# A planned last stage: banks counted as taken, and the planner's constants set anew

## The chip, the cores and the metric

One core of a Trainium2 chip. The metric is device time in microseconds of one execution; smaller is better. TensorE does matrix products, VectorE and ScalarE elementwise work with access to the accumulator memory PSUM (eight banks, each 128 partitions x 512 fp32), GpSimd elementwise work in SBUF only, SyncE issues the transfers.

## The reference

Three layers, one after the other, on 3072 tokens of width 512, fp32 in and out:

```python
attn  = softmax(mask(q @ k.T / 8)) @ v          # 4 batches, 8 heads, window 128 and 4 sinks
x     = attn as (3072, 512)
d     = softmax(x @ phi, over tokens)           # 32 slots
slots = relu((d.T @ x)[e] @ w1[e]) @ w2[e]      # 8 experts, 4 slots each
x     = softmax(x @ phi, over slots) @ slots
h     = x @ w_in                                # (512, 2048)
out   = (h - tanh(h)) @ w_out                   # (2048, 512)
```

## The kernel before

Attention and the experts come first and are written out by hand; the change leaves them alone. The last stage computes `out`, transposed, in three chunks of 1024 tokens. Because x is a combination of 32 slots, h for a tile of 128 of the 2048 columns (an f of 16) and 512 tokens is a single matmul (L1554) of a small precomputed matrix with the slot weights `cT`. What is large is the product with `w_out`. Each fp32 operand is split into a rounded part and a residual (`gh` and `gl` for activations, `whi` and `wlo` for weights), and three of the four cross products are summed.

The work on one tile of h, each step one instruction on 128x512:

1. TensorE makes h in one of four PSUM banks: `h0`, `h1`, `y`, `cvt` (L1554).
2. ScalarE takes tanh in place (L1565) and a scaled square into `u` (L1566).
3. VectorE multiplies the two (L1313), back into the bank or out into a spare buffer (`w`, `wf`, `g`, `cv` and others).
4. ScalarE casts the result to `gh` (L1623).
5. `gl` is the rest (L1477): by VectorE if the source is a bank, by GpSimd if it is a buffer.
6. TensorE multiplies into the accumulators `a0` to `a3` (named `o` in the profile, L1485).

The first chunk of 1024 tokens runs as 32 regular units of twelve matmuls (4 blocks of output rows x 3 cross products), called "r". The second and third run by a scheme with seven products in place of eight of half size (`MULT`: P1 to P7): a unit is one product for one f, six matmuls, and units of two products alternate (`PAIRS`). Its operands are four tiles for each i of 8 (`A11`, `A12`, `A21`, `A22`) and their sums `S1` to `S4`, made by VectorE (L1477) from banks and buffers. A bank with A22, A11 or A12 is thus read by ScalarE (cast) and by VectorE (sums, residual), and comes free when the last reader is done. On the weight side sums of `w_out` blocks are needed too (`T1` to `T4`); those for T3 and T4 are made once in the first chunk, while the last weights are still being converted and split, and those for T1 and T2 are split afresh (`trhi`, `trlo`) when they are used.

The regular units up to the sixth are written out by hand. From 256 us on the order is planned by a program at build time, in two steps:

- A loop over a heap of dated events (`produce`, `act`, `mul`, `cast`, `ssum`, `unit`, `t_fresh`) gives out banks, buffers and the five `gh`/`gl` pairs, and enters each instruction as a task with a wanted time `at`. The constants set these times, in planned us: h is asked for `LEAD` ahead of its unit (L1561, `push(max(at + 0.3, due[gs[j + 1]] - LEAD), ...)`), the cast of a regular tile `RCAST` and that of a sum `SCAST` ahead, the split of a T1 or T2 weight `TCAST` ahead. The weight sums for T3 and T4 come `TLAG` after the conversion of their weight, the last three `TLAG2` later each.
- `_Order.emit` lists the tasks: again and again it takes, over all engines, the task that can start first by its planned durations (`US`), and of those that could start at the same moment on one engine the one with the smallest `at`. A task can start when those that it depends on are done (dependencies are kept by name of bank or buffer: a read waits for the write before, a write for the write and all reads before). Two readers of one bank have no dependency. The order in which tasks were taken is the order in which the instructions stand in the engines' queues, which are in order. `BUSY` and `shared` stand for engines still at work from before and for sums that VectorE and GpSimd can't run side by side.

What waits for what at run time is then set by semaphores that the framework puts in from the tiles' reads and writes, not by the planner.

Of the kernel before, what the change touches and what calls it, by code (L numbers as in the profile page):

```python
# [19 lines left out]
PSUM = bass.MemoryType.PSUM  # L20
# [37 lines left out]
CT = ((1, 0), (1, 1), (1, 2))  # L58
EPS_T = 0.0
US = {"tanh": 0.49, "mm": 0.2276, "h": 0.232, "act": 1.1, "cast": 0.49, "cast2": 0.3, "v": 0.6, "vs2": 0.34, "p": 1.26, "p2": 0.7, "pc": 0.7, "pch": 0.38, "ev": 0.49, "sq": 0.56}  # L60
LEAD, RCAST, SCAST, TCAST = 10.0, 7.0, 4.5, 6.0
RPS = 11
GGAP = 1.4
TLAG = 14.0
TLAG2 = 2.0
PAIRS = (((1, "P4"), (1, "P5")), ((1, "P7"), (1, "P1")), ((1, "P6"), (1, "P2")), ((1, "P3"), (2, "P4")),
         ((2, "P5"), (2, "P1")), ((2, "P7"), (2, "P6")), ((2, "P2"), (2, "P3")))
# [78 lines left out]
class _Order:  # L146

    LAT = {"PE": 0.2, "SP": 4.0, "ACT": 0.11, "DVE": 0.09, "POOL": 0.05}
    SELF = {"ACT": 0.12, "DVE": 0.12, "POOL": 0.12}
    BUSY = {"ACT": 0.3, "DVE": 2.7, "POOL": 3.8}  # L150

    def __init__(self):
# [12 lines left out]
    def emit(self, near_end=0, mark=None, busy=True):  # L165
        tasks = sorted(self.tasks, key=lambda t: t[:2])
        n = len(tasks)
        wrote, read = {}, {}
        deps, users = [set() for _ in tasks], [[] for _ in tasks]
        for k, (_, _, _, rd, wr) in enumerate(tasks):  # L170
            for b in rd:
                if b in wrote:
                    deps[k].add(wrote[b])
            for b in wr:
                if b in wrote:
                    deps[k].add(wrote[b])
                deps[k] |= read.get(b, set())
            for b in rd:
                read.setdefault(b, set()).add(k)
            for b in wr:  # L180
                wrote[b], read[b] = k, set()
        for k, d in enumerate(deps):
            d.discard(k)
            for j in d:
                users[j].append(k)
        left = [len(d) for d in deps]
        avail, free = [{} for _ in tasks], dict(self.BUSY) if busy else {}
        ready = {k for k in range(n) if not left[k]}
        order, port = [], 0.0
        while len(order) < n:  # L190
            best = None
            engs = {e for k in ready for e in tasks[k][2]}
            for eng in engs:
                t0 = free.get(eng, 0.0)
                at = {}
                for k in ready:
                    if eng in tasks[k][2]:
                        x = max([t0] + [v if e != eng else v - 0.06 - self.LAT.get(e, 0.0) + self.SELF.get(e, 0.0) for e, v in avail[k].items()])
                        if self.shared(tasks[k], eng) and x < port:
                            x = port if eng == "POOL" or x < port - 0.08 else port + 0.02  # L200
                        at[k] = x
                first = min(at.values())
                k = min(k for k in at if at[k] <= first + EPS_T)
                c = (at[k], tasks[k][2][eng][0], eng, k)
                best = c if best is None else min(best, c)
            t, us, eng, k = best
            ready.remove(k)
            free[eng] = t + us
            if self.shared(tasks[k], eng):
                port = t + us  # L210
            done = t + us + 0.06 + self.LAT.get(eng, 0.0)
            order.append((k, eng))
            for j in users[k]:
                avail[j][eng] = max(avail[j].get(eng, 0.0), done)
                left[j] -= 1
                if not left[j]:
                    ready.add(j)
            self.log.append((t, us, eng, tasks[k][0], tasks[k][3], tasks[k][4]))
        for x, (k, eng) in enumerate(order):
            if mark and n - x == near_end:  # L220
                mark()
            tasks[k][2][eng][1]()
# [5 lines left out]
def tile_kernel(ctx: ExitStack, tc: tile.TileContext, qk, vv, v0, v0t, nw, phi, w1, w2,  # L228
# [17 lines left out]
    def run(ctx, fast):  # L246
# [1540 lines left out]
        for s, todo in plan.items():  # L1787
# [3 lines left out]
            for e, (f, ph) in enumerate(todo):  # L1791
# [12 lines left out]
                else:  # L1804
# [7 lines left out]
                    if f >= 8:  # L1812
# [6 lines left out]
                        def tsub(at, d, dn, a, b, rd):  # L1819
                            arith(at, d, a, b, rd, dn, half=True)  # L1820

                        tb += TLAG if f < 13 else TLAG + TLAG2 * (f - 12)
                        tsub(tb, B1[:, lo_], [l_], B1[:, hi_], B1[:, lo_], [r_, l_])
# [130 lines left out]
```

## Time and profile before

| | |
|---|---|
| median of 3 runs | 516.47 us (516.26 to 517.09) |
| the profiled execution | 516.18 us |
| its span, first to last instruction | 514.4 us |
| TensorE busy | 484.3 us, 94% of the span |
| VectorE busy | 420.5 us, 82% |
| ScalarE busy | 384.6 us, 75% |
| GpSimd busy | 297.4 us, 58% |

The profile names the engines PE (TensorE; PEld its weight loads), DVE (VectorE), ACT (ScalarE), POOL (GpSimd) and SP (SyncE). A row of the timeline gives start, duration, engine, line, operation, output<-inputs by name with the buffer number left out, and the idle time of the engine just before with what ended it. Matmuls are pipelined: each shows about 0.4 us, but the next may start 0.23 us later.

### The profile page before, as it was taken

What the parts mean: (1) busy time and instruction counts of PE and PEld (TensorE: products, weight loads), DVE (VectorE), ACT (ScalarE), POOL (GpSimd) and SP (SyncE); (2) the same over time, 40 slices, a digit from 0 to 9 for tenths busy, and PEclk for the clock granted to TensorE, in tenths of its full rate; (3) what the DMA queues carried; (4) which work ended last, traced back from release to release, by engine and by line L of the source; (5) the groups of instructions that cost most, each with busy time, mean ns of one, the idle gap of its engine ahead of it and who ended that gap; (6) DMA issues with size and microseconds to landing.
All of it is one profiled execution on the core that took longest, in us unless ns stands there. A gap on an engine that the chain in (4) does not pass through costs nothing. (4 is left out here: it accounts for less than half of the span.)

```text
span 514.4 us, 10274 instructions
## 1 busy us (share of the span) xinstructions
PE 484.3 (94%) x3554; PEld 334.8 (65%) x3554; DVE 420.5 (82%) x841; ACT 384.6 (75%) x1088; POOL 297.4 (58%) x362
## 2 busy tenths in 40 slices
PE   8799999899998999799999999999999999999995
PEld 4565565555555633236788788888788778878784
DVE  2999998898988559678999999788967887883983
ACT  4989998998999414238897887898866898574751
POOL 0466755765744100014999996167645884579952
PEclk9999999999999999999999999999999999999998
DMA  8989977442385899992432001120000030100022
GB/s 297 413 320 349 362 273 252 150 142 94 114 287 183 312 326 409 410 408 95 148 98 82 1 0 43 41 83 1 1 0 0 2 123 1 41 1 1 1 83 85
DMA packets 21996, 77.60 MB, mean 151 GB/s; under 512 B 2867, under 2 KB 4019, under 8 KB 20019
## 3 DMA queue, kind: packets, MB, share of 16 engines
q1 hardware_dynamic: 21938, 76.89, 40.6%
q8 instruction: 29, 0.48, 0.4%
q14 instruction: 29, 0.23, 0.1%
HBM read 70.59 MB, written 6.29 MB: 149 GB/s over the span
## 5 line engine op out<-in xcount | busy, mean ns | idle before, releaser
L1485 PE MATMUL o<-gh,whi 128*128 128x512 f32 x232 | 91.9, 396 | 0.0
L1485 PE MATMUL o<-gh,wlo 128*128 128x512 f32 x232 | 91.1, 393 | 0.0
L1485 PE MATMUL o<-gl,whi 128*128 128x512 f32 x232 | 71.3, 391 | 0.0
L705 POOL TENSOR_TENSOR w<-w,su 128x528 f32<-128x528 f32 x38 | 41.4, 1090 | 51.1 <-DVE su L702 36.2
L1477 POOL TENSOR_TENSOR gl<-w,gh 128x512 fp32r<-128x512 f32 x39 | 51.0, 1316 | 30.0 <-ACT gh L1623 28.6
L695 ACT ACTIVATE w<-w,nb 128x132 f32<-128x132 f32 x152 | 59.6, 393 | 1.2
L1485 PEld LDWEIGHTS o<-gh,whi 128*128 128x128 f32 x232 | 43.7, 188 | 11.1 <-ACT mk L1683 0.4
L1485 PEld LDWEIGHTS o<-gl,whi 128*128 128x128 f32 x232 | 43.6, 188 | 9.8 <-DVE gl L1477 0.2
L1485 PEld LDWEIGHTS o<-gh,wlo 128*128 128x128 f32 x232 | 43.7, 188 | 9.5
L759 PE MATMUL av<-w,w 128*64 128x256 f32 (+1 forms) x448 | 48.3, 344 | 0.0
L665 PE MATMUL sc<-w 64*64 64x200 f32 (+2 forms) x768 | 44.5, 332 | 2.0 <-DMA w<-in_qk 1.1
L1138 POOL TENSOR_SCALAR whi<-wx 128x512 fp32r<-128x512 f32 x6 | 3.7, 618 | 59.9 <-DVE wx L136 59.9
L759 PEld LDWEIGHTS av<-w,w 128*64 128x64 f32 x448 | 25.9, 136 | 16.4 <-issue 10.7
L665 PEld LDWEIGHTS sc<-w 64*64 64x64 f32 x768 | 25.9, 132 | 15.0 <-issue 10.3
L1623 ACT CAST gh<-h 128x512 fp32r<-128x512 f32 x37 | 21.8, 588 | 18.1 <-DVE h L1313 7.3
L679 ACT COPY w<-sc 128x264 f32<-128x264 f32 x63 | 21.2, 374 | 13.7 <-PE sc L795 6.3
L741 DVE TENSOR_TENSOR w<-pT,c_t 128x512 f32<-128x512 f32 x46 | 31.3, 680 | 0.0
L1313 DVE TENSOR_TENSOR h<-u,h 128x512 f32<-128x512 f32 x37 | 25.4, 687 | 5.3 <-ACT u L1566 5.3
L727 PE MATMUL pT<-c_t,w 128*128 128x128 f32 x148 | 23.5, 281 | 6.4 <-POOL w L705 5.7
L1477 DVE TENSOR_TENSOR gl<-h,gh 128x512 fp32r<-128x512 f32 x37 | 25.4, 685 | 4.9 <-ACT gh L1623 4.4
L1623 ACT CAST gh<-w 128x512 fp32r<-128x512 f32 x39 | 24.0, 622 | 7.0 <-PE o L1485 5.9
L1565 ACT ACTIVATE h<-h 128x512 f32<-128x512 f32 x46 | 27.1, 592 | 2.1 <-PE h L1554 2.0
(391 smaller groups left out, 1339.7 us busy)
## 6 DMA issues: line engine op xcount, KB each, us to landing
w<-in_w SPq DMA_DIRECT2D x32, 512.0 KB, 10.2
w<-in_w SPq DMA_DIRECT2D x14, 1024.0 KB, 6.8
w<-in_qk SPq DMA_DIRECT2D x16, 780.0 KB, 6.6
w<-in_w_out SPq DMA_DIRECT2D x15, 512.0 KB, 3.6
w<-in_vv SPq DMA_DIRECT2D x16, 384.0 KB, 3.9
w<-in_w_in SPq DMA_DIRECT2D x8, 512.0 KB, 4.8
out<-xt SPq DMA_DIRECT2D x12, 256.0 KB, 2.0
win_t<-in_w_in SPq DMA_DIRECT2D x4, 512.0 KB, 9.9
```

Of the source, the lines that this page charges most:

```text
L665: PE.matmul(sc_t[i][u][w, o:o + n], a[r, 64 * j:64 * j + 64], kslc(a, lo, n)[r, :], start=True, stop=True)
L679: ACT.copy(z, base)
L695: ACT.activation(Z[:, u, :], Z[:, u, :], AF.Exp, bias=nb[:, u:u + 1], scale=SCALE, accum_out=su[:, u, :])
L705: (POOL if i < NQ - 1 else DVE).tensor_tensor(Z, Z, su.to_broadcast([P, 4, CH]), op=ALU.mult)
L727: PE.transpose(pt[:, P * u:P * u + P], Z[:, u, 0:P], ident)
L741: DVE.tensor_tensor(d[:, :, 0, :], src, mL, op=ALU.mult)
L759: PE.matmul(dst[r, :], v[:, t, r], l, start=start, stop=stop, skip_group_check=True)
L1313: DVE.tensor_tensor(g, u, h, op=ALU.mult)
L1477: td.any_of(at, {e: (us[e], lambda e=e: names[e].tensor_tensor(dst, a, b, op=alu), len(engs) > 1 or sbuf) for e in engs}, rd, wr)
L1485: PE.matmul(o, w, a, start=start, stop=stop)
L1565: add(at, "ACT", US["tanh"], [b[1]], [b[1]], lambda: ACT.activation(b[0], b[0], AF.Tanh, scale=ca))
L1623: add(at, "ACT", US["cast"], [gn], [f"gh{x}"], lambda: ACT.copy(gh_b[x], g))
```

## The change

Four of the constants on two lines get other values, three of the seven stay: `LEAD` 10 to 13, `RCAST` 7 to 6, `SCAST` 4.5 to 3, `TLAG` 14 to 6. And `emit` keeps, for each PSUM bank and engine, when the last task that reads the bank on that engine is done; a task on another engine that reads the bank can't start sooner in the plan.

```diff
-LEAD, RCAST, SCAST, TCAST = 10.0, 7.0, 4.5, 6.0
+LEAD, RCAST, SCAST, TCAST = 13.0, 6.0, 3.0, 6.0
 RPS = 11
 GGAP = 1.4
-TLAG = 14.0
+TLAG = 6.0
 TLAG2 = 2.0
@@ class _Order
     SELF = {"ACT": 0.12, "DVE": 0.12, "POOL": 0.12}
+    PSUM = ("a0", "a1", "a2", "a3", "h0", "h1", "y", "cvt")
     BUSY = {"ACT": 0.3, "DVE": 2.7, "POOL": 3.8}
@@ def emit
-        order, port = [], 0.0
+        order, port, seen = [], 0.0, {}
         while len(order) < n:
...
                         x = max([t0] + [v if e != eng else v - 0.06 - self.LAT.get(e, 0.0) + self.SELF.get(e, 0.0) for e, v in avail[k].items()])
+                        for b in tasks[k][3]:
+                            if b in self.PSUM:
+                                x = max([x] + [v for e, v in seen.get(b, {}).items() if e != eng])
                         if self.shared(tasks[k], eng) and x < port:
...
             done = t + us + 0.06 + self.LAT.get(eng, 0.0)
+            for b in tasks[k][3]:
+                if b in self.PSUM:
+                    seen.setdefault(b, {})[eng] = done
             order.append((k, eng))
```

## Rows read from the trace of the kernel before

**Rows 1.** Busy time by stretch of the planned stage (us; instructions in brackets).

```profile
256.10:330.00 73.90, 73.90 (x321) 59.69 (x320) 68.87 (x112) 60.87 (x119) 60.59 (x73) 1.00 0.15 50
330.00:420.00 90.00, 87.12 (x375) 69.94 (x374) 72.61 (x114) 74.02 (x140) 61.18 (x64) 1.00 0.08 30
420.00:509.00 89.00, 88.18 (x381) 70.53 (x379) 66.02 (x97) 57.58 (x104) 61.45 (x61) 1.00 0.07 25
```

Columns: stretch, its length, then PE, PEld, DVE, ACT, POOL, granted clock, DMA share, GB/s.

**Rows 2.** The end of the chain that ended last (start, us, what).

```profile
508.35 1.37 DVE xt L1477 x2
```

**Rows 3.** Waits of TensorE, 270 to 515 us (us in total, times, longest).

```profile
PE h L1554 <- DVE w L1313: 1.2, 1, 1.2
PE y L1554 <- DVE w L1313: 0.9, 1, 0.9
PE o L1485 <- POOL gl L1477: 0.8, 2, 0.5
PE y L1554 <- DVE gl L1477: 0.7, 1, 0.7
```

**Rows 4.** Timeline around 409 us, and the stretch 400 to 410 by engine.

```profile
399.45 0.59 ACT L1623 CAST gh<-h 128x512 fp32r<-128x512 f32 x1 [1.11 <-DVE cv L1477]
...
408.12 0.40 PE L1554 MATMUL y<-cT,wst 96*128 96x512 f32 x1
...
409.04 0.68 DVE L1313 TENSOR_TENSOR w<-u,h 128x512 f32<-128x512 f32 x1
...
409.77 0.50 PE L1554 MATMUL h<-cT,wst 96*128 96x512 f32 x1 [1.25 <-DVE w L1313]
...
400.00:410.00 10.00, 8.76 (x38) 6.84 (x37) 8.11 (x13) 9.45 (x19) 7.57 (x10) 1.00 0.00 1
```

**Rows 5.** Timeline around 413 us.

```profile
412.20 0.60 ACT L1623 CAST gh<-cvt 128x512 fp32r<-128x512 f32 x1
...
412.64 0.62 PE L1485 MATMUL o<-gl,whi 128*128 128x512 f32 x2
...
412.83 0.69 DVE L1477 TENSOR_TENSOR w<-w,cvt 128x512 f32<-128x512 f32 x1 [0.73 <-ACT gh L1623]
...
413.44 0.68 DVE L1313 TENSOR_TENSOR w<-u,y 128x512 f32<-128x512 f32 x1
...
414.17 0.50 PE L1554 MATMUL y<-cT,wst 96*128 96x512 f32 x1 [0.91 <-DVE w L1313]
```

**Rows 6.** Timeline around 456 us.

```profile
454.23 0.58 ACT L1623 CAST gh<-h 128x512 fp32r<-128x512 f32 x1 [1.20 <-DVE wf L1477]
...
456.52 1.29 POOL L1477 TENSOR_TENSOR gl<-wf,gh 128x512 fp32r<-128x512 f32 x1 [0.91 <-ACT gh L1623]
...
457.17 0.39 PE L1485 MATMUL o<-gh,trlo 128*128 128x512 f32 x1
...
457.86 0.50 PE L1485 MATMUL o<-gl,trhi 128*128 128x512 f32 x1 [0.30 <-POOL gl L1477]
```

**Rows 7.** Timeline around 361 us.

```profile
359.93 0.39 PE L1485 MATMUL o<-gh,trlo 128*128 128x512 f32 x1
...
360.16 0.39 PE L1485 MATMUL o<-gl,trhi 128*128 128x512 f32 x1
...
361.27 0.50 PE L1554 MATMUL y<-cT,wst 96*128 96x512 f32 x1 [0.72 <-DVE gl L1477]
```

**Rows 8.** Timeline around 484 us.

```profile
483.93 0.39 PE L1485 MATMUL o<-gh,trlo 128*128 128x512 f32 x1
...
484.81 0.50 PE L1485 MATMUL o<-gl,trhi 128*128 128x512 f32 x1 [0.50 <-POOL gl L1477]
```

**Rows 9.** Groups of instructions, 270 to 515 us (busy us, mean ns | idle before <-releasers).

```profile
L1477 POOL TENSOR_TENSOR gl<-w,gh 128x512 fp32r<-128x512 f32 x39 | 51.0, 1316 | 30.0 <-ACT gh L1623 28.6 <-PE o L1485 1.4
...
L1623 ACT CAST gh<-h 128x512 fp32r<-128x512 f32 x36 | 21.2, 588 | 18.1 <-DVE h L1313 7.3 <-DVE w L1477 5.4 <-PE o L1485 2.1
```

**Rows 10.** Groups of instructions of VectorE, 256 to 330 us.

```profile
L1477 DVE TENSOR_TENSOR wlo<-w,whi 128x512 fp32r<-128x512 f32 x1 | 2.3, 2331 | 0.1
```

## The prediction

> **What bounds the kernel now.** I read the busy time by stretch first, then the chain that ended last, then the waits of TensorE alone, and last the timeline around each of those waits. In the stretches [rows 1] the reader is to see that the stage which the change touches, from 256.1 us on, is TensorE's: it is busy 73.90 of 73.90 us in the first third, 87.12 of 90.00 in the second and 88.18 of 89.00 in the third, with a granted clock of 1.00 in all three. No other engine is near that in the second and third. In the first third VectorE, with 68.87 of 73.90 us, is nearly as full. The chain ends on VectorE's two sums after the last matmul [rows 2], which the change leaves where they are. So a new order can win only TensorE's holes. The list of its waits [rows 3] adds up to 3.6 us in five events. Each is seen in the timeline, where the loss is the time from start to start less the 0.23 us at which matmuls follow each other undisturbed (359.93 to 360.16 in [rows 7]):
>
> - at 409.77: 1.65 from 408.12, less 0.23, is 1.42 us [rows 4]
> - at 414.17: 1.53 from 412.64, less two matmuls, is 1.07 us [rows 5]
> - at 457.86: 0.69 from 457.17, less 0.23, is 0.46 us [rows 6]
> - at 361.27: 1.11 from 360.16, less 0.23, is 0.88 us [rows 7]
> - at 484.81: 0.88 from 483.93, less 0.23, is 0.65 us [rows 8]
>
> Together that is 4.48 us, the ceiling of this change but for the restart: the matmul after a wait shows 0.50 where its neighbours show 0.40 [rows 4], so 0.1 us each, 0.5 us for five.
>
> **The change part by part.** It removes and adds no operation. The same matmuls, casts, sums and transfers are emitted; each task's engine (where it has a choice) and its place in the queues come from a planner whose picture is edited. The SyncE queue gets its output transfers where the sums end, as before. So all is a matter of who stands in front of whom.
>
> *The bank rule.* Until now the planner lets ScalarE's cast of a bank and VectorE's sum out of the same bank run side by side. The trace shows that they don't. ScalarE's casts out of the h banks lost 5.4 us to VectorE's sums (w) [rows 9], though such a cast reads none of their results; and VectorE's sum at 412.83 sat 0.73 us until the cast at 412.20 was through [rows 5]. As queues are in order, what stands behind such a wait is late by as much. I follow the five holes back:
>
> - 414.17. VectorE's sum of cvt waits 0.73 us for the cast of cvt, and right behind it stands the product w<-u,y, which empties the bank that TensorE wants. A planner that knew would have run the product, or the two other reads, meanwhile. The hole would go whole: 1.07 us.
> - 409.77. TensorE waits for the product at 409.04. ScalarE, which feeds it, lost 1.11 us at 399.45 to the same cause, and between 400 and 410 it is busy 9.45 of 10 us [rows 4], so it never makes that up. I count the 1.42 us as won.
> - 457.86. TensorE waits for GpSimd's residual at 456.52, which waited 0.91 us for its cast, which stood behind a cast that waited 1.20 us for VectorE's sum out of its own bank [rows 6]. Won: 0.46 us.
> - 361.27 waits for a residual of VectorE and 484.81 for one of GpSimd [rows 7, 8], engines that in the timeline work without a pause ahead of it. The rule doesn't touch them: 0.
>
> That is 2.95 us. Against it: all queues are dealt anew, and a planner whose times are a little off makes new holes. The trace shows five in this stage; I charge one of the mean size, 4.48 / 5 = 0.90 us. Bounds: none (0) and all five again (4.48). I take one: the first third shows that a planned order can hold 74 us without a hole [rows 1], and the two holes outside the rule's reach show that one more is to be expected.
>
> *LEAD 10 to 13.* The 86 matmuls that make h are asked for 3 planned us sooner. They wait for one of four banks, so mostly nothing moves. Best case: VectorE gets ahead and the 0.88 us hole goes [rows 7]. Worst case: one more matmul stands at the head of TensorE's queue before its bank is free, with all products behind it; the three holes of this kind average (1.42 + 1.07 + 0.88) / 3 = 1.12 us. Between -0.88 and +1.12 I take 0.
>
> *RCAST 7 to 6, SCAST 4.5 to 3.* The casts lose rank against the tanh and square of later tiles. Behind a cast of an S operand come its own 0.59 us and 1.32 us on GpSimd [rows 9], 1.91 us before TensorE can use it. With 4.5 planned us that left 2.6, now 1.1. Best case 0, since the holes traced to a late residual are paid above; the worst is a rival. I take 0.
>
> *TLAG 14 to 6.* The sums for the last weights are asked for 8 planned us sooner, in the third that has no hole to win, so the gain is 0. What hides them is that TensorE's weights are ready ahead of use. If that cover goes, a weight residual on VectorE comes late; the nearest row is the one that took 2.33 us [rows 10], where a VectorE sum of the same 128x512 takes 0.69 [rows 5], so 1.64 us. Between 0 and +1.64 I take 0, since in the trace these sums already run as soon as the engines have room.
>
> The Trainium skill has a rule that speaks against this part (SBUF — State Buffer, "Who interferes with whom"): a VectorE sum with both inputs in SBUF and a GpSimd operation that reads SBUF exclude each other for a whole instruction. The 2.33 us row agrees with it, and by it the term would be 1.64 us a collision rather than 0.
>
> **Sum.** The profiled execution took 516.18 us: a span of 514.40 and 1.78 around it, which stays. 516.18 - 2.95 + 0.90 = 514.13. The median of the runs, 516.47, is 0.29 above that execution, so I forecast **514.4 us**.
>
> **The rivals.**
>
> *All holes go.* Then 516.18 - 4.48 - 0.5 + 0.29 = 511.5 us. For it speaks that three are of one kind; against it that 361.27 and 484.81 are of another. Chance 0.12.
>
> *The holes move.* The planner sees the bank and shifts the pause from one queue to another; TensorE still waits for a bank as long. The banks are four before and after, which speaks for it; that ScalarE and VectorE have 16 us of 90 free in the second third [rows 1], and so room, speaks against. Time 516.5. Chance 0.14.
>
> *The early weight sums collide.* One collision in the first third comes through to TensorE: 514.13 + 1.64 + 0.29 = 516.1, no change again. For it speaks the full VectorE, against it that TensorE lost nothing there while one collision did happen. This is the exclusion that the skill's page on SBUF names. Chance 0.08.
>
> *Slower: late residuals of the S operands.* 64 products use an S operand whose cast now has 1.1 planned us to spare in place of 2.6. The two holes of that kind measure 0.46 and 0.65 us, 0.56 in the mean. If one in eight of the 64 waits as long, that is 8 x 0.56 = 4.5 us, less the 2.95 won: 516.18 + 1.5 + 0.29 = 518.0. It decides from the sixth such wait on (2.95 / 0.56 = 5.3). For it speaks that GpSimd stood behind a cast at 456.52; against it that rank counts only where two tasks are ready at once. Chance 0.24.
>
> **How the numbers follow.** The forecast has 0.42. The range runs from 511.5, all holes gone, to nine late residuals: 516.18 + 9 x 0.56 - 2.95 + 0.29 = 518.6; what lies beyond I put under 0.2. The forecast's own range, with no new hole or with two, is 513.5 to 515.3. A measurement of this kernel can tell about 0.2%, 1.0 us, from no change. Faster: 0.42 + 0.12 = 0.54. Same: 0.14 + 0.08 = 0.22. Slower: 0.24.
>
> **What would show it.** Right: ScalarE's idle before casts of h, y and cvt put down to VectorE's sums falls from several us to under 2, TensorE's waits for VectorE in the second third are gone, and its busy time there goes from 87.12 of 90.00 to 89 or more, with the first third still without a hole. Wrong: TensorE's waits name GpSimd's gl in more than five places (the slower rival), or the weight residuals wlo (the collision), or stay at 3 us with other names (the holes move).

## The result and the profile after

The changed kernel takes 510.47 us (median of 6 runs, 509.47 to 512.03), the kernel before 516.59 (516.26 to 517.09): a ratio of 0.9879, 95% interval 0.9865 to 0.9892. That is 6.1 us faster. I had forecast 514.4 us and a range from 511.5 to 518.6, so the direction was right, the gain was three times what I had forecast (2.05 us), and the time lies 1 us under the range.

The busy time of the changed kernel by stretch, with the columns of [rows 1]; the last stretch ends at 504 because the last matmul starts at 503.31 in place of 508.60:

```profile
256.10:330.00 73.90, 73.90 (x322) 60.31 (x322) 69.25 (x115) 64.89 (x126) 63.40 (x75) 1.00 0.15 50
330.00:420.00 90.00, 90.00 (x392) 73.31 (x392) 73.45 (x118) 75.68 (x143) 64.53 (x68) 1.00 0.08 30
420.00:504.00 84.00, 83.70 (x367) 68.27 (x365) 62.58 (x91) 54.22 (x96) 60.32 (x60) 1.00 0.07 26
```

TensorE is now busy in the whole of the first two stretches, where the second showed 87.12 of 90.00 before; the 0.30 us missing from the third are its end. The other engines are busy as long as before to within 5 us.

Of TensorE's waits [rows 3] none is left. The list of all waits from 258 to 506 us has nothing longer for it than these two of its weight loads (us in total, times, longest):

```profile
PEld cvt L1561 <- DVE wf L1320: 0.2, 1, 0.2
PEld o L1492 <- ACT u L1573: 0.2, 1, 0.2
```

The groups that answer to [rows 9] are these (seven lines were added above them in the code, so L1477 is now L1484 and L1623 is L1630):

```profile
L1484 POOL TENSOR_TENSOR gl<-w,gh 128x512 fp32r<-128x512 f32 x39 | 51.1, 1318 | 26.5 <-ACT gh L1630 16.8 <-PE o L1492 9.7
...
L1630 ACT CAST gh<-h 128x512 fp32r<-128x512 f32 x38 | 22.4, 589 | 11.2 <-DVE w L1484 4.2 <-DVE h L1320 2.6 <-PE o L1492 2.4
```

GpSimd's residuals now wait 16.8 us for their casts rather than 28.6. ScalarE's casts out of `h` still wait 4.2 us for VectorE's sums into `w`, hardly less than the 5.4 before. Taken over the casts of `h`, `y` and `cvt` and over all sums, read one by one from the timeline, these waits fall from 17.8 us (17 casts) to 7.2 (7 casts); I come back to that.

What the new order looks like where one bank is read by both engines shows in the timeline around 402 us. There is one bank `y`: VectorE sums out of it at 401.23, ScalarE casts it at 402.55, VectorE takes the residual at 403.17 (VectorE's rows first, then ScalarE's).

```profile
401.23 0.68 DVE L1484 TENSOR_TENSOR g<-y,g 128x512 f32<-128x512 f32 x1
401.82 0.69 DVE L1320 TENSOR_TENSOR h<-u,h 128x512 f32<-128x512 f32 x1
402.55 0.69 DVE L1484 TENSOR_TENSOR w<-w,h 128x512 f32<-128x512 f32 x1
403.17 0.69 DVE L1484 TENSOR_TENSOR gl<-y,gh 128x512 fp32r<-128x512 f32 x1
...
402.55 0.59 ACT L1630 CAST gh<-y 128x512 fp32r<-128x512 f32 x1
```

The three reads of `y` follow each other, and in the gap VectorE has a product and a sum of another bank, with no idle time. At 412.83 in the kernel before it stood still at a sum of this kind [rows 5].

### The profile page after: what moved, and what is told of

The parts are those of the page before. It is cut to its first block, busy times and chain, and to the rows that moved or that the text cites. A ratio compares the mean times of both kernels' runs of the same rounds, so it can differ in the third digit from the quotient of the medians.

```text
span 509.0 us, 10286 instructions
## 1 busy us (share of the span) xinstructions
PE 481.4 (95%) x3554; PEld 335.6 (66%) x3554; DVE 416.6 (82%) x838; ACT 386.0 (76%) x1087; POOL 301.0 (59%) x366
## 4 chain that ended last, share of the span: by engine, by line
PE 61%; DVE 14%; DMA 12%; POOL 5%; ACT 5%; issue 1%; SPq 0%; POOLq 0%; DVEq 0%; ACTq 0%
PE o L1492 44%; DMA w<-in_w 8%; DVE mx L693 3%; PE av L766 2%; DVE w L748 2%; PE sc L672 2%; ACT w L702 2%; PE h L1561 2%; PE pT L734 2%; DMA w<-in_w_out 2%; POOL w L712 2%; DMA w<-in_w_in 1%; PE mi L530 1%; DVE w L687 1%; POOL gl L1306 1%
## 5 line engine op out<-in xcount | busy, mean ns | idle before, releaser
L1484 POOL TENSOR_TENSOR gl<-w,gh 128x512 fp32r<-128x512 f32 x39 | 51.1, 1318 | 26.5 <-ACT gh L1630 16.8
L1320 DVE TENSOR_TENSOR h<-u,h 128x512 f32<-128x512 f32 x40 | 27.6, 691 | 10.1 <-ACT u L1573 9.9
L1630 ACT CAST gh<-h 128x512 fp32r<-128x512 f32 x40 | 23.5, 589 | 11.2 <-DVE w L1484 4.2
L1630 ACT CAST gh<-w 128x512 fp32r<-128x512 f32 x39 | 24.2, 621 | 7.7 <-PE o L1492 7.4
L1484 DVE TENSOR_TENSOR gl<-h,gh 128x512 fp32r<-128x512 f32 x40 | 27.4, 685 | 2.7 <-ACT gh L1630 2.1
L702 ACT ACTIVATION_READ_ACCUMULATOR w<-w,nb 128x1 f32 x152 | 28.4, 187 | 0.0
## 6 DMA issues: line engine op xcount, KB each, us to landing
w<-in_w SPq DMA_DIRECT2D x32, 512.0 KB, 10.2
```

What stands on the lines that cost most here:

```text
L702: ACT.activation(Z[:, u, :], Z[:, u, :], AF.Exp, bias=nb[:, u:u + 1], scale=SCALE, accum_out=su[:, u, :])
L1320: DVE.tensor_tensor(g, u, h, op=ALU.mult)
L1484: td.any_of(at, {e: (us[e], lambda e=e: names[e].tensor_tensor(dst, a, b, op=alu), len(engs) > 1 or sbuf) for e in engs}, rd, wr)
L1630: add(at, "ACT", US["cast"], [gn], [f"gh{x}"], lambda: ACT.copy(gh_b[x], g))
```

## Where the time went: an account of the stage

From the start of the first planned matmul to the start of the last, the stage took 252.42 us before (256.18 to 508.60) and 245.78 after (257.53 to 503.31), with the same matmuls: 6.64 us less. The five holes that I had read make 4.48 of it, their restarts 0.5. The rest is mostly pauses that I had not counted. This is one of them, in the timeline of the kernel before:

```profile
366.88 0.61 PE L1485 MATMUL o<-gl,whi 128*128 128x512 f32 x2
...
367.50 0.19 PEld L1554 LDWEIGHTS h<-cT,wst 96*128 96x128 f32 x1 [0.43 <-DVE gl L1477]
367.50 0.50 PE L1554 MATMUL h<-cT,wst 96*128 96x512 f32 x1
...
367.84 0.39 PE L1485 MATMUL o<-gh,whi 128*128 128x512 f32 x1
```

The row of the matmul shows no idle time, since the matmul before it is drawn 0.39 us long and covers the wait; only the weight load has a bracket. But from start to start it is 0.62 for two matmuls in place of 0.46, and 0.34 in place of 0.23 for the next, so 0.27 us are lost. The kernel before has 17 steps of 0.27 to 0.40 us between neighbours, 1.65 us above 0.23 in sum (the five restarts are among them), and 0.27 us more in front of pairs drawn as one row. After the change there is one such step, 0.09 us. 4.48 + 1.65 + 0.27 - 0.09 = 6.31 of the 6.64 us; the other 0.3 I don't place.

Where the stage starts varies between executions (256.1 to 259.0 us in the profiles of this study) although nothing ahead of it is changed, so the length of the stage is the steadier measure beside the medians.

## The experiments

Three theories stood at the start. **R**: the holes come from reads of one bank that the planner lets overlap and that run one after the other on the chip, so that a queue stands where the plan has it going on. **L**: it is the earlier request of h, which gives the engines more to work ahead on. **C**: the order before was unlucky, and any new deal of the queues is likely to be better. Later **S** joined: a plan with more air in it is better, whatever the air is put into.

One number comes from the planner itself, not from the chip: in the list of planned starts and lengths, how many times a read of a bank on one of ScalarE and VectorE starts inside a read of the same bank on the other. Every plan here has TensorE without a pause for 244.0 planned us; this number is what I compare.

| kernel | overlapping reads planned (us) | stage on the chip, us | median, us | ratio to before, 95% interval |
|---|---|---|---|---|
| before | 36 (10.3) | 252.4 | 516.59 | |
| changed | 0 | 245.8 | 510.47 | 0.9879 [0.9865, 0.9892] |
| e1: rule alone | 0 | 247.3 | 511.88 | 0.9898 [0.9881, 0.9914] |
| e2: constants alone | 7 (2.2) | 246.2 | 510.72 | 0.9875 [0.9858, 0.9892] |
| e3: LEAD 13 alone | 7 (2.0) | 247.0 | 511.00 | 0.9886 [0.9869, 0.9902] |
| e4: changed, casts back | 0 | 246.6 | 511.25 | 0.9898 [0.9875, 0.9921] |
| e5: LEAD 11 alone | 9 (2.2) | 247.2 | 511.70 | 0.9900 [0.9884, 0.9917] |
| e6: LEAD 10, others new, no rule | 35 (9.9) | 251.8 | 516.35 | 0.9995 [0.9983, 1.0007] |
| e7: LEAD 8, no rule | 38 (10.2) | 254.3 | 519.24 | 1.0035 [1.0023, 1.0048] |
| e8: rule, LEAD 8 | 0 | 246.2 | 510.53 | 0.9881 [0.9858, 0.9905] |
| e9: rule for ScalarE | 14 (2.3) | 248.0 | 512.41 | 0.9911 [0.9895, 0.9928] |
| e10: rule for VectorE | 18 (5.5) | 249.2 | 513.51 | 0.9946 [0.9925, 0.9967] |
| e11: longer hand-over, no rule | 38 (10.1) | 250.7 | 515.00 | 0.9965 [0.9952, 0.9978] |
| e12: changed, TLAG back | 0 | 246.1 | 510.74 | 0.9878 [0.9859, 0.9897] |

The times of before beside which the ratios stand were 516.80 (e1 to e4), 517.14 (e5 to e8) and 516.82 us (e9 to e12).

### e1 to e3: either half alone

```diff
 # e1: the changed kernel
-LEAD, RCAST, SCAST, TCAST = 13.0, 6.0, 3.0, 6.0
+LEAD, RCAST, SCAST, TCAST = 10.0, 7.0, 4.5, 6.0
-TLAG = 6.0
+TLAG = 14.0
```

> The bank rule alone, with the constants of before. Theory R (the holes came from two readers of one bank that the planner thought could run at once): nearly all of the gain comes with the rule, 510 to 512 us, TensorE's waits in the second and third thirds under 1 us. Theory L (the earlier requests, LEAD 13, make the gain by giving the engines more to work ahead on): 515 to 517 us. Theory C (any new deal of the queues lands somewhere else, no part is the cause): any value between 509 and 518, not ordered by either.

```diff
 # e2: the kernel before
-LEAD, RCAST, SCAST, TCAST = 10.0, 7.0, 4.5, 6.0
+LEAD, RCAST, SCAST, TCAST = 13.0, 6.0, 3.0, 6.0
-TLAG = 14.0
+TLAG = 6.0
```

> The four new constants alone, without the bank rule. Theory R: most holes stay, 514 to 517 us, and ScalarE's casts of h, y and cvt still wait several us for VectorE's sums. Theory L: 510 to 512 us. Theory C: anywhere between 509 and 518.

```diff
 # e3: the kernel before
-LEAD, RCAST, SCAST, TCAST = 10.0, 7.0, 4.5, 6.0
+LEAD, RCAST, SCAST, TCAST = 13.0, 7.0, 4.5, 6.0
```

> The kernel before with LEAD 13 in place of 10 and nothing else. Theory R: 514 to 517 us. Theory L: within 1 us of the run with all four constants. If that run is fast and this one is not, the cast or weight constants matter. Theory C: no relation between the two.

All three are fast, 511.88, 510.72 and 511.00 us. Each half alone brings nearly the whole gain, and together they bring no more. That fits none of the theories as I had put them: R had no place for e2 and e3 (both were to stay above 514 us), L none for e1, and C fits anything. The plans gave the clue. LEAD 13 without the rule has only 7 overlapping reads where LEAD 10 has 36, so the two halves may take away the same thing in two ways. That is R again, in a form that can be tested: the number of overlapping reads decides, not the edit that sets it.

### e4 and e12: the other constants back

```diff
 # e4: the changed kernel
-LEAD, RCAST, SCAST, TCAST = 13.0, 6.0, 3.0, 6.0
+LEAD, RCAST, SCAST, TCAST = 13.0, 7.0, 4.5, 6.0
```

> The changed kernel with RCAST 7 and SCAST 4.5 as before. Theory R and theory L alike: within 1 us of the changed kernel, 510 to 511.5 us, since rank alone among ready tasks moves little. Theory C: it may land anywhere up to 517.

```diff
 # e12: the changed kernel
-TLAG = 6.0
+TLAG = 14.0
```

> The changed kernel with TLAG 14 as before. Theories R and S: 510 to 511.5 us, no difference to the changed kernel, since nothing in the first third waits for the early weight sums. If the weight sums matter, the first third shows holes and 512 or more.

511.25 and 510.74 us, with intervals that overlap that of the changed kernel. RCAST, SCAST and TLAG are worth nothing that these times can tell. The traces hint at a little for the casts: with RCAST 7 and SCAST 4.5 beside LEAD 13, e4 and e3 each have one hole in the first third (0.66 us, at 269.51 and 269.75, behind ScalarE's copy of an accumulator) that the changed kernel and e2 do not have, and their stages are 0.8 us longer. That is one profiled execution of each.

### e5 to e8: the number of overlaps against the distance

```diff
 # e5: the kernel before
-LEAD, RCAST, SCAST, TCAST = 10.0, 7.0, 4.5, 6.0
+LEAD, RCAST, SCAST, TCAST = 11.0, 7.0, 4.5, 6.0
 # e6: the kernel before
-LEAD, RCAST, SCAST, TCAST = 10.0, 7.0, 4.5, 6.0
+LEAD, RCAST, SCAST, TCAST = 10.0, 6.0, 3, 6.0
...
-TLAG = 14.0
+TLAG = 6.0
 # e7: the kernel before
-LEAD, RCAST, SCAST, TCAST = 10.0, 7.0, 4.5, 6.0
+LEAD, RCAST, SCAST, TCAST = 8.0, 7.0, 4.5, 6.0
 # e8: the changed kernel
-LEAD, RCAST, SCAST, TCAST = 13.0, 6.0, 3.0, 6.0
+LEAD, RCAST, SCAST, TCAST = 8.0, 7.0, 4.5, 6.0
...
-TLAG = 6.0
+TLAG = 14.0
```

> The kernel before with LEAD 11 in place of 10, nothing else. The plan of before has 36 reads of a bank in which one engine's read starts inside another's (10.3 us of overlap), the one with LEAD 13 has 7 (2.2), the one with LEAD 11 has 9 (2.2): the number falls in one step. Theory R (the holes come from reads planned to overlap that the chip runs one after the other): 510 to 512 us. Theory L (each planned us of earlier request helps by itself): a third of the way, 514 to 515.5 us. Theory C (any new deal): anywhere.

> The kernel before with RCAST 6, SCAST 3 and TLAG 6 as changed, but LEAD 10, without the rule: 35 overlapping reads in the plan (9.9 us). Theory R: 515.5 to 517.5 us, as before. Theory L: the same, 515.5 to 517.5. Theory C: the queues are dealt anew, so it lands with the others at 510 to 512.

> The kernel before with LEAD 8, without the rule: 38 overlapping reads in the plan (10.2 us). Theory R: 515.5 to 518 us, as before. Theory L: 517.5 to 522, slower than before. Theory C: anywhere.

> The bank rule with LEAD 8 and the other constants of before: no overlapping read in the plan, h asked for 2 planned us later than before. Theory R: 510.5 to 512.5 us, as with the rule and LEAD 10. Theory L: 516 to 521, slower than the rule with LEAD 10. Theory C: anywhere.

These four tell the theories apart. One planned us more of LEAD (e5) brings 1.00%, where L wanted a third of that. e6 changes three constants, deals the queues anew and keeps the overlaps, and the time doesn't move: 0.9995. C has no room for that. Of its TensorE waits, from 258 to 512 us, the two longest are those of [rows 3], and the third has the same size and releaser, with `cvt` in place of `y`:

```profile
PE h L1554 <- DVE w L1313: 1.2, 1, 1.2
PE y L1554 <- DVE w L1313: 0.9, 1, 0.9
PE cvt L1554 <- DVE gl L1477: 0.7, 1, 0.7
PE o L1485 <- DVE h L1477: 0.4, 1, 0.4
PE o L1485 <- POOL gl L1477: 0.2, 1, 0.2
```

With LEAD 8 the rule decides between 519.24 us (e7) and 510.53 (e8). e8 asks for h 5 planned us later than the changed kernel, with the other constants of before, and has its time; against e1, from which it differs in LEAD alone (8 in place of 10), it is not slower either. Its stretches show TensorE about as full:

```profile
256.10:330.00 73.90, 73.90 (x322) 60.17 (x322) 67.93 (x114) 60.46 (x116) 60.72 (x72) 1.00 0.16 50
330.00:420.00 90.00, 90.00 (x392) 73.45 (x391) 74.59 (x119) 76.75 (x147) 64.27 (x67) 1.00 0.08 30
420.00:504.00 84.00, 83.20 (x364) 67.87 (x362) 61.57 (x93) 55.15 (x99) 61.68 (x60) 1.00 0.07 26
```

So between 8 and 13 LEAD has no effect that shows where the plan has no overlaps. Where it has, less LEAD does cost something: e7 is slower than R said (515.5 to 518) and lies in the range of L (517.5 to 522); the number of overlaps, 38 against 36, doesn't explain that. Its waits have spread to the products, behind late casts and residuals:

```profile
PE o L1485 <- DVE gl L1477: 1.5, 2, 0.8
PE o L1485 <- ACT gh L1623: 1.1, 1, 1.1
PE o L1485 <- POOL gl L1477: 0.6, 1, 0.6
PE h L1554 <- DVE w L1313: 0.5, 1, 0.5
```

### e9 and e10: the rule one engine at a time

```diff
 # e1 with
-                            if b in self.PSUM:
+                            if eng == "ACT" and b in self.PSUM:   # e9; e10: "DVE"
```

> The rule for ScalarE's tasks alone, constants of before: a cast may not start in the plan while VectorE reads its bank, but VectorE's sums may still start inside a cast. 14 overlapping reads stay (2.3 us in place of 10.3). Theory R: 511 to 513.5 us, and what waits are left are VectorE's for a cast. Theory S (a plan with more air is what helps, whatever the air is put into): like the run with longer hand-over times. Theory C: anywhere.

> The rule for VectorE's tasks alone: a sum may not start in the plan while ScalarE reads its bank, but a cast may still start inside a sum. 18 overlapping reads stay (5.5 us in place of 10.3). Theory R: between the rule for ScalarE and the kernel before, 512 to 515 us, with ScalarE's casts waiting for VectorE's sums. Theory C: anywhere.

512.41 and 513.51 us: with 14 and 18 overlaps (2.3 and 5.5 us) between 0 and 36, in that order, as R has it. They also test two holes one by one. I had put the hole at 409.77 down to ScalarE's wait at 399.45 for a VectorE sum [rows 4], and that at 414.17 to VectorE's wait for a cast [rows 5]. With the rule for VectorE alone the first must stay and the second go. In the timeline of e10 the first is there to the hundredth, with the same ScalarE wait ahead of it:

```profile
399.08 0.59 ACT L1630 CAST gh<-h 128x512 fp32r<-128x512 f32 x1 [1.10 <-DVE cv L1484]
...
407.75 0.40 PE L1561 MATMUL y<-cT,wst 96*128 96x512 f32 x1
409.40 0.50 PE L1561 MATMUL h<-cT,wst 96*128 96x512 f32 x1 [1.24 <-DVE w L1320]
```

1.65 us from start to start, less 0.23, is the same 1.42 us. At 413.80, where the second was, TensorE loses 0.15 us. The first is the only TensorE wait in e10's list; from start to start smaller ones show, 0.23 us at 346.93 and 0.29 at 360.90:

```profile
PE h L1561 <- DVE w L1320: 1.2, 1, 1.2
```

With the rule for ScalarE alone it must be the other way round. The first is gone, and the second is there, smaller: VectorE's sum of cvt waits 0.51 us for the cast of cvt, and TensorE loses 0.42 us (0.88 from the start of the pair at 410.56, less two matmuls) in place of 1.07:

```profile
410.10 0.69 DVE L1484 TENSOR_TENSOR w<-w,cvt 128x512 f32<-128x512 f32 x1 [0.51 <-ACT gh L1630]
...
410.56 0.63 PE L1492 MATMUL o<-gl,whi 128*128 128x512 f32 x2
410.71 0.68 DVE L1320 TENSOR_TENSOR w<-u,y 128x512 f32<-128x512 f32 x1
...
411.44 0.50 PE L1561 MATMUL y<-cT,wst 96*128 96x512 f32 x1 [0.25 <-DVE w L1320]
```

The other hole of e9, 0.51 us at 482.10, is behind a VectorE sum, as in e1.

### e11: air of another kind

```diff
 # the kernel before
-    LAT = {"PE": 0.2, "SP": 4.0, "ACT": 0.11, "DVE": 0.09, "POOL": 0.05}
+    LAT = {"PE": 0.2, "SP": 4.0, "ACT": 0.31, "DVE": 0.29, "POOL": 0.25}
```

> The kernel before, without the rule, but with 0.2 us more planned hand-over time after every task of ScalarE, VectorE and GpSimd: 38 overlapping reads in the plan (10.1 us), more air between a producer and its consumer. Theory R: 514.5 to 518 us, near before. Theory S: 510 to 512.5 us.

515.00 us, 0.35% faster than before, with 38 overlaps in its plan. More air helps a little and brings a third of what the rule alone brings (e1, 1.02%). S is not the cause, though it isn't nothing.

### What the missing rule costs in each plan

The number of overlaps doesn't say what they cost: e11 and e7 both have 38 and lie 4.2 us apart. The plans can be asked for the cost. This is a calculation on the plans with the planner's own durations, made after the runs, and not a run: each engine's tasks keep their order, and are timed once more with the bank rule in force, each reader of a bank waiting for those on another engine that stand before it in the plan's order. With the rule left out TensorE has no pause in any of them; with it TensorE gets these:

| plan | pauses of TensorE with the rule in force, us | stage on the chip, longer than the changed kernel's by, us |
|---|---|---|
| e7: LEAD 8, no rule | 8.3 | 8.5 |
| e6: LEAD 10, others new, no rule | 5.8 | 6.0 |
| before | 5.5 | 6.6 |
| e11: longer hand-over, no rule | 4.9 | 4.9 |
| e10: rule for VectorE | 3.3 | 3.4 |
| e9: rule for ScalarE | 0.9 | 2.2 |
| e5: LEAD 11 alone | 0.7 | 1.4 |
| e2, e3: LEAD 13, no rule | 0.5, 0.5 | 0.4, 1.2 |
| changed, e1, e4, e8, e12 | 0 | 0 to 1.5 |

So R holds in a sharper form: what decides is how long the order makes TensorE wait once the reads of a bank take turns. It places e7, which the count of overlaps did not. In the plan of before the pauses stand at the same matmuls as four of the five holes: 0.71 us at that of 361.27, 1.34 at 409.77, 1.16 at 414.17 and 0.80 at 484.81, where the chip lost 0.88, 1.42, 1.07 and 0.65. Not all agrees. The hole at 457.86 is not among them, and the calculation has pauses of 0.43 and 0.52 us for matmuls at 480.93 and 482.88 that lost 0.11 us at most. In other plans too it has late pauses that the chip does not show, the longest 0.80 us in e10.

## Why the prediction was wrong, point by point

- **The mechanism of the rule was right, its size was not.** The bank rule alone is worth 1.0%. The time falls with the planned overlaps in steps: 0 to 9 of them go with 510.5 to 511.9 us, 14 and 18 with 512.4 and 513.5, 35 to 38 with 515.0 to 519.2. Two holes were traced to the right engine, as e9 and e10 show. The forecast was a gain of 2.95 less 0.90, 2.05 us, where the stage got 6.64 shorter. Of the 4.59 us between, 1.53 are two holes counted at 0, 0.90 the new hole that did not come, and 1.83 short pauses (1.65 + 0.27 - 0.09) that were not in the sum; 0.3 I don't place.
- **The ceiling was mis-sized, and with it the lower end of the range.** I wrote that the five waits in TensorE's list, 4.48 us, with 0.5 for the restarts, are the ceiling. The pauses come to 4.48 + 1.65 + 0.27 = 6.4 us. The short ones stand in no list of waits of the matmuls; of their kind I had counted only the five restarts, and 1.4 us were left out. This is why the time lies under the range.
- **The two holes at 361.27 and 484.81 were counted as out of the rule's reach, at 0.** They went too, 1.53 us, and in e8 with the rule and LEAD 8 as well; e1 lost both and had one of 0.52 us at 483.88, at another matmul, behind a VectorE sum. I had followed each back by one step, to an engine that works without a pause just ahead. Timed once more with the rule in force, the plan of before has pauses at these very matmuls, 0.71 and 0.80 us, so they come from the missing rule as the others do. Which single wait starts each is open. In the kernel before ScalarE's casts lost 1.8 us to VectorE's sums (g) between 340 and 361 us; in e10 the same two casts wait as long (0.44 and 1.34 us) and 0.29 of the 0.88 us hole is left, so they are not the whole of the first.
- **The hole at 457.86, 0.46 us, I counted as the rule's.** It went with it, but the calculation does not have it, so for this one the cause is argued only.
- **The new hole, 0.90 us, did not come.** The plans that have the whole rule hold: in the changed kernel, e8 and e12 TensorE loses nowhere more than 0.2 us, and e1 and e4 have one hole each (0.52 and 0.66 us).
- **The constants at 0 each.** Right on top of the rule, as far as the times can tell: e8, e4 and e12 show no difference for LEAD, the casts and TLAG. For LEAD without the rule it was wrong by far: e3 measures 1.14%, 5.8 us, where I had the bounds at -0.88 and +1.12. I had looked at which engine gets ahead; what LEAD does is decide whether the planner's order has overlaps. Since both halves remove the same holes, the change as a whole was not mis-sized by it; that was luck.
- **The rivals.** "All holes go", at 511.5 us and 0.12, is what happened, and with the short pauses it goes 1 us lower. The holes did not move to other names, and there were no late residuals of the S operands. The early weight sums did not collide at TensorE's cost: the first third of the changed kernel has no hole, and a 128x512 residual on VectorE took 1.00 us in place of 2.33 [rows 10]. The exclusion that the Trainium skill states (SBUF — State Buffer, "Who interferes with whom") did not reach the path.
- **What would show it.** I had said that ScalarE's waits for VectorE's sums before casts of h, y and cvt fall to under 2 us. They fall from 17.8 to 7.2. VectorE's waits of its sums for a cast fell from 5.9 us over the stage to 0.5. A wait that the plan contains seems to stand where nothing else was due and to cost nothing: in e2 ScalarE's casts of banks wait 9.0 us for VectorE's sums, and TensorE has no hole. The waits that cost are those that an order gets only when the rule comes into force. The calculation on the plans speaks for this; no run tests it by itself.

Left open: why the plan falls from 36 overlaps to 9 between LEAD 10 and 11. No run here beats the changed kernel, and by this account an order can hardly win more: its stage has 0.1 us of pauses left. e2, e8 and e12 have its time within their intervals.

## What to carry to other kernels

Where an order is planned at build time, compare what the plan lets run at once with what the traces show one after the other. Here the missing rule showed as waits between two engines that have no data to hand over, and its price appeared later and elsewhere, in a queue that is in order: 10 us after ScalarE's wait for the hole at 409.77. A count of such clashes is a first sign; the order timed once more with the rule in force gives the price. Read the loss of a pipelined engine from start to start, not from its list of idle times: here 30% of it stood in short pauses that the list of the matmuls' waits doesn't name. And when two edits each bring the whole gain, look for the one quantity that both change before calling it luck.

## What was not expected of the hardware

That two engines which only read one PSUM bank wait for each other was seen before the change [rows 5]; its price was not expected: a plan with 36 overlaps, 10.3 us in all, has a stage of 252.4 us, and the rule alone takes 5.1 off it (e1). The Trainium skill (PSUM — Partial Sum Buffer, "PSUM bank collisions raise a hardware error") says that the compiler back end orders any two instructions on different engines that touch the same bank and 32 partitions, reads against reads included. The wait of 0.73 us at 412.83 agrees with it, and in none of the fourteen traces does a read of `y` or `cvt` by ScalarE overlap one by VectorE from 262 us on. No run here let the two read at once, so what the chip would make of it is not shown. A matmul's row is 0.39 us long while the next may start 0.23 us after it, so by these two numbers a wait of up to 0.16 us leaves no idle time in the row; at 367.50 only the weight load shows it.
